# An attention-and-MLP kernel on one core: tail products take PSUM banks in the order of their release, and the list scheduler adds a constant to its assumed cost of every query/key eviction

## The chip, the cores and the metric

The kernel runs on one core of a Trainium2 chip. The metric is the device time of one execution in microseconds (us). A comparison is made in rounds in which both kernels run on the same chip. Each run is listed with the mean clock that the throttle granted to TensorE; 1.000 is full speed. A run over 1.5% above the fastest of its kernel is "slow"; a ratio compares fast runs alone, a median is over all runs. Engine names are those of the profile: PE is TensorE's matmul, PEld its weight load, ACT is ScalarE, DVE is VectorE. L1109 means line 1109 of the kernel.

## The reference, cut to what matters

```python
x: (1, 2048, 640), H = 32 heads of 20
xn  = layernorm(x)
q, k, v = split(xn @ wqkv)                       # 640 x 1920
p   = softmax(q @ k^T * 20**-0.5)                # 32 x 2048 x 2048 exponentials
s   = (p @ v) @ wo                               # 640 x 640
h   = layernorm(xn)
y   = gelu(h^T @ w1 + b1) @ w2 + b2              # mixes along the sequence, F = 1536
out = x + s * silu(y^T)
```

## The kernel before: the parts that the change and the argument touch

The kernel is not written in instruction order. A list scheduler, run when the kernel is built, deals all steps to the engines. It keeps a clock for each engine, reckoned with assumed costs. At each turn it asks every engine for candidates (priority, ready time, action), takes the engine whose next candidate is ready first, and emits that engine's candidate of lowest priority number. The compiled program is the resulting fixed list.

First, the costs decide which engine gets an eviction ("ev" step), and in which order everything after it is dealt:

```python
def dv(n, rate=1.04):  return 75.0 + n * rate          # believed DVE cost, ns
def ac(n):             return 90.0 + n * 0.833 + 60.0  # believed ACT cost, ns

def do_step(j, eng):
    s = j.steps[j.i]; j.i += 1
    if s[0] == "ev":
        n = s[8]; fn = ev_fn(s, eng)
        cost = ac(n) if eng == "act" else dv(n, 0.55 if s[7].startswith("xTe") else 1.04)
        getattr(pr, eng)(fn, reads=s[5], writes=s[6], name=s[7], cost=cost)
    # ... matmul steps and the rest
```

Second, PE's candidates. A score block (L1109: two 512-wide matmuls of 32 rows for one exponential, often with a third for a DVE chain) has priority 0. Filler work (value products L755, query/key chunks L722, MLP products L810, output products L879) has 30 and more. Attention-value products (L1224) have 8.

Third, the tail. The last two output blocks (`LBS`) are accumulated in PSUM banks named in advance, and each product waits for "its" bank to come free:

```python
BA, BB = (5, 7), (4, 0)          # bank of the 512-wide part, bank of the 128-wide part
for i, b in enumerate(LBS):
    add_job(f"tpa{i}", ... op_mms(b, ps(BA[i]), 0, 512, bank_slot[BA[i]], True, False) ..., rq + (f"bankoff{BA[i]}",), 60.0 + i)
    add_job(f"tpb{i}", ... op_mms(b, ps(BB[i], 128), 512, 128, ...) ..., rq + (f"bankoff{BB[i]}",), 60.0 + i)
...
if not bankq and 7 not in busybanks and 7 not in bank_off:
    bank_off.add(7); done.add("bankoff7")          # the same for the ACT and DVE banks
```

## Time and profile before

| what | before | how it is read |
|---|---|---|
| time, median of six runs | 867.07 us (866.84 to 868.54) | the runs taken beside the changed kernel |
| profiled span, clock | 865.0 us, 1.000 | page, list of cores |
| start of the 27th exponential | 46.19 us | timeline of ACT |
| **middle**: from there to the end of the last exponential | 809.2 us | 855.38 - 46.19 |
| **end**: from there to the end of the span | 9.6 us | 865.0 - 855.38 |

The three stretches add up to the span, so every difference between two kernels has one of three addresses. The words "start", "middle" and "end" are used in this sense throughout. The lines that carry these numbers stand in the prediction.

### The profile page before, as it was taken

How to read it: one execution, taken by the hardware profiler on the slowest of the kernel's cores; microseconds unless marked ns; L12 is line 12 of the kernel's file. 1: busy time of each engine (PE TensorE's matmuls, PEld its weight loads, DVE VectorE, ACT ScalarE, POOL GpSimd, SP SyncE). 2: the span in 40 equal slices, each digit the busy share in tenths (PEclk: the TensorE clock that was granted, in tenths of full speed). 3: DMA queues.
4: the chain of work that ended last, by engine and by line, in shares of the span. 5: the costliest groups of instructions: out<-in, count | busy, mean ns of one | idle time of the engine just before them, and what ended most of it. 6: DMA issues, size and time to landing. Idle time of an engine off the chain costs nothing.

```text
span 865.0 us, 16498 instructions
## 1 busy us (share of the span) xinstructions
PE 797.6 (92%) x5828; PEld 256.1 (30%) x5918; DVE 823.6 (95%) x2047; ACT 845.4 (98%) x925; POOL 14.0 (2%) x23
## 2 busy tenths in 40 slices
PE   8899999999999999999999999999899998998997
PEld 5422222222222223222322222222222222232233
DVE  8989999999999999999999999999999999999996
ACT  7899999999999999999999999999999999999996
POOL 3200000000000000000000000000000000000000
PEclk9999999999999999999999999999999999999999
DMA  8141010011010323010013022123312201042111
GB/s 236 48 113 30 9 35 10 16 36 31 11 55 14 77 36 88 11 55 10 16 25 78 23 51 52 25 52 71 67 30 46 47 11 11 3 102 69 41 39 41
DMA packets 123350, 39.32 MB, mean 45 GB/s; under 512 B 84312, under 2 KB 122152, under 8 KB 123272
## 3 DMA queue, kind: packets, MB, share of 16 engines
q1 hardware_dynamic: 123272, 38.27, 19.4%
q8 instruction: 50, 0.82, 0.4%
q14 instruction: 28, 0.23, 0.1%
HBM read 25.88 MB, written 9.83 MB: 41 GB/s over the span
## 4 chain that ended last, share of the span: by engine, by line
ACT 87%; PE 9%; DVE 2%; POOL 1%; issue 1%; ACTq 0%; POOLq 0%
ACT pt_sb L1137 85%; PE ps_all L1109 3%; PE ps_all L1224 1%; ACT zt_sb L843 1%; PE ps_all L755 1%; PE ps_all L879 1%; ACT zt_sb L838 1%; PE ps_all L1704 1%; DVE ew_sb L1177 0%; PE ps_all L683 0%; PE ps_all L722 0%; POOL v_sb L1298 0%; PE ps_all L703 0%; DVE dpt_sb L1183 0%; PE ps_all L658 0%
## 5 line engine op out<-in xcount | busy, mean ns | idle before, releaser
L1137 ACT ACTIVATE pt_sb<-ps_all 128x1024 bf16<-128x1024 f32 x888 | 819.9, 1147 | 3.6 <-PE ps_all L1109 3.0
L1109 PE MATMUL ps_all<-qk_sb 32*128 32x512 bf16 (+1 forms) x2112 | 367.8, 377 | 48.3 <-ACT pt_sb L1137 36.7
L1177 DVE TENSOR_SCALAR ew_sb<-ps_all 128x512 uint16<-128x512 uint16 x272 | 184.2, 684 | 20.7 <-PE ps_all L1109 19.6
L1109 PEld LDWEIGHTS ps_all<-qk_sb 32*128 32x128 bf16 x2112 | 97.1, 91 | 347.0 <-ACT pt_sb L1137 299.9
L1183 DVE SCALAR_TENSOR_TENSOR dpt_sb<-ps_all,el_sb 128x512 uint16<-128x512 f32 x272 | 182.0, 684 | 1.8
L1224 PE MATMUL ps_all<-pt_sb,v_sb 128*32 128x512 bf16 (+1 forms) x1833 | 162.6, 378 | 0.3 <-issue 0.3
L1181 DVE TENSOR_TENSOR el_sb<-ev_sb,el_sb 128x512 bf16<-128x512 bf16 x272 | 111.0, 417 | 1.1
L1182 DVE TENSOR_TENSOR el_sb<-el_sb,ew_sb 128x512 bf16<-128x512 bf16 x272 | 110.2, 417 | 0.9
L1224 PE MATMUL ps_all<-dpt_sb,v_sb 128*32 128x512 bf16 (+1 forms) x279 | 83.7, 379 | 0.0
L810 PE MATMUL ps_all<-regB,regA 128*128 128x128 bf16 (+1 forms) x371 | 75.6, 300 | 2.9 <-issue 1.1
L1178 DVE TENSOR_SCALAR ev_sb<-ew_sb 128x512 bf16<-128x512 uint16 x272 | 75.3, 285 | 2.3
L810 PE MATMUL ps_all<-regC,regA 128*128 128x128 bf16 (+1 forms) x370 | 74.2, 300 | 1.8 <-issue 1.0
L1179 DVE TENSOR_SCALAR el_sb<-ew_sb 128x512 bf16<-128x512 uint16 x272 | 75.1, 284 | 0.0
L722 PE MATMUL ps_all<-xnT_sb,wqk_sb 128*112 128x512 bf16 x200 | 68.2, 405 | 0.4 <-DVE zt_sb L816 0.4
L1224 PEld LDWEIGHTS ps_all<-pt_sb,v_sb 128*32 128x32 bf16 x1833 | 35.4, 94 | 55.6 <-issue 50.2
L1696 PE MATMUL ps_all<-wrm_sb 128*128 128x512 bf16 (+1 forms) x117 | 34.0, 376 | 3.9 <-DVE ps_all L513 2.2
L810 PEld LDWEIGHTS ps_all<-regB,regA 128*128 128x128 bf16 x384 | 25.8, 97 | 39.1 <-issue 24.0
L810 PEld LDWEIGHTS ps_all<-regC,regA 128*128 128x128 bf16 x384 | 25.0, 97 | 39.8 <-issue 28.1
L1704 PE MATMUL ps_all<-wrm_sb,v_sb 128*128 128x512 bf16 x97 | 34.0, 385 | 1.3 <-issue 0.7
L755 PE MATMUL ps_all<-wv_sb,xnT_sb 128*128 128x160 bf16 (+1 forms) x160 | 33.7, 303 | 0.4 <-DVE pk_sb L1030 0.3
L879 PE MATMUL ps_all<-wo_sb,xnT_sb 128*128 128x128 bf16 (+3 forms) x151 | 30.2, 298 | 1.1 <-issue 0.5
L722 PEld LDWEIGHTS ps_all<-xnT_sb,wqk_sb 128*112 128x112 bf16 x200 | 20.7, 127 | 30.5 <-issue 13.4
(89 smaller groups left out, 354.4 us busy)
## 6 DMA issues: line engine op xcount, KB each, us to landing
regA<-in_B_w_dram SPq DMA_DIRECT2D x6, 1024.0 KB
regA<-in_B_w_dram SPq DMA_DIRECT2D x8, 768.0 KB
qkT_scratch_dram<-pk_sb SPq DMA_DIRECT2D x40, 112.0 KB
qk_sb<-qkT_scratch_dram SPq DMA_DIRECT2D x56, 80.0 KB
regA<-in_A_x_dram SPq DMA_DIRECT2D x6, 640.0 KB
on_scratch_dram<-on_sb SPq DMA_DIRECT2D x124, 20.0 KB
out_dram<-regC SPq DMA_DIRECT2D x3, 640.0 KB
wqk_sb<-in_A_wqkv_dram SPq DMA_DIRECT2D x2, 680.0 KB
```

The lines of the kernel that those rows point to most:

```text
L722: steps.append(("pe", lambda e, dc=dc: e.matmul(ps_all[0:112, bk * 512:(bk + 1) * 512], wqk_sb[:, dc * 1280 + c0:dc * 1280 + c0 + 112], xn ...
L810: steps.append(("pe", lambda e, k=k: e.matmul(ps(bk, n), wap[:, k, col0:col0 + 128], rows[:, k, c0:c0 + n], start=(k == 0), stop=(k == nk ...
L1109: pr.pe(lambda e, outp=outp, lhsT=lhsT, rhs=rhs, g=g: e.matmul(outp, lhsT, rhs, start=True, stop=True, tile_position=(32 * g, 0)), reads=q ...
L1137: tk = pr.act(lambda e: e.activation(outp, inp, AF.Exp, bias=-self.OFFS * math.log(2.0) / 128.0, scale=math.log(2.0) / 128.0), reads=[bank ...
L1177: (lambda e: e.tensor_scalar(w3, lo, 0x7FFF, None, ALU.bitwise_and), bs, [sw], dv(N)),
L1178: (lambda e: e.tensor_scalar(v_, w_, 1.0 / 256.0, -128.0, ALU.mult, ALU.add), [sw], [sv], dv(N, .26)),
L1179: (lambda e: e.tensor_scalar(l_, w_, a3 / 65536.0, (b3 - 64.0 * a3) / 256.0, ALU.mult, ALU.add), [sw], [sl_], dv(N, .26)),
L1181: (lambda e: e.tensor_tensor(l_, v_, l_, ALU.mult), [sv, sl_], [sl_], dv(N, .52)),
L1182: (lambda e: e.tensor_tensor(l_, l_, w_, ALU.mult), [sl_, sw], [sl_], dv(N, .52)),
L1183: (lambda e: e.scalar_tensor_tensor(o_, zr, -(self.OFFS - 16256.0), l_, ALU.add, ALU.add), bs + [sl_], [S_(f"dpt{s0 + i}") for i in range( ...
L1224: pr.pe(lambda e, outp=outp, lhsT=lhsT, rhs=rhs, k=k, g=g: e.matmul(outp, lhsT, rhs, start=(k == 0), stop=(k == NB - 1), tile_position=(0, ...
L1704: pe_full(lambda e: e.matmul(ps(AB), zero, wrm_sb[:, P:P + 512], start=new, stop=new), [S_("warm"), S_("v_ones")], [sl_acc], "warmz", 512)
```

## The change

It has two parts. **Tail banks**: the tail products no longer wait for named banks; each takes the next bank that comes free. **Cost**: a query/key eviction is reckoned 130 ns dearer, on either engine. For 512 columns that makes 707 ns on ACT, where the trace of before has a record of 784 (at 30.00 us, with the next operation queued behind it, that one starts 661 ns later), and 737 on DVE, where it has 810. The intent is a shorter tail and a start in which evictions go to the engine that is really free.

```diff
-        BA, BB = (5, 7), (4, 0)
+        tbank = []
 ...
-            add_job(f"tpa{i}", (... op_mms(b, ps(BA[i]), ...)), rq + (f"bankoff{BA[i]}",), 60.0 + i)
+            add_job(f"tpa{i}", (... op_mms(b, ps(tbank[2 * i]), ...)), rq + (f"tbank{2 * i}",), 60.0 + i)
 ...
+        def bank_out(b):
+            bank_off.add(b)
+            tbank.append(b)
+            done.add(f"tbank{len(tbank) - 1}")
 ...
                 cost = ac(n) if eng == "act" else dv(n, 0.55 if s[7].startswith("xTe") else 1.04)
+                if s[3] in ("q", "k"):
+                    cost += 130.0
 ...
-                    bank_off.add(7)
-                    done.add("bankoff7")
+                    bank_out(7)
```

(Cut: the same replacement of `BA`, `BB` by `tbank` in the last steps of each block, and of `bank_off.add` by `bank_out` for the other banks.)

More of the change, by code (lines that the diff above doesn't have):

```diff
@@ L1456, in schedule @@
             add_job(f"stl{b0}", storel_steps(b0, nb), tuple(f"res{b}" for b in range(b0, b0 + nb)), 30.0)
-        BA, BB = (5, 7), (4, 0)
+        tbank = []
         def tail_fin(i):
             b = LBS[i]
-            steps = op_mms(b, ps(BA[i]), 0, 512, bank_slot[BA[i]], False, True)
-            steps += op_mms(b, ps(BB[i], 128), 512, 128, bank_slot[BB[i]], False, True)
+            steps = op_mms(b, ps(tbank[2 * i]), 0, 512, bank_slot[tbank[2 * i]], False, True)
+            steps += op_mms(b, ps(tbank[2 * i + 1], 128), 512, 128, bank_slot[tbank[2 * i + 1]], False, True)
             z = ztmp(i)
             g = regC[:, b, :]
-            steps.append(("act", lambda e: e.activation(z[:, 512:640], ps(BB[i], 128), AF.Copy), [bank_slot[BB[i]]],
+            steps.append(("act", lambda e: e.activation(z[:, 512:640], ps(tbank[2 * i + 1], 128), AF.Copy), [bank_slot[tbank[2 * i + 1]]],
                           [S_(f"z{i}_1")], f"tz{b}b", ac(128)))
             if i == 0:
-                steps.append(("dve", lambda e: e.tensor_tensor(g[:, 0:512], ps(BA[i]), g[:, 0:512], ALU.mult),
-                              [bank_slot[BA[i]], S_(f"g{b}")], [S_(f"r{b}_0")], f"tp{b}a", dv(512)))
+                steps.append(("dve", lambda e: e.tensor_tensor(g[:, 0:512], ps(tbank[2 * i]), g[:, 0:512], ALU.mult),
+                              [bank_slot[tbank[2 * i]], S_(f"g{b}")], [S_(f"r{b}_0")], f"tp{b}a", dv(512)))
                 steps.append(("dve", lambda e: e.tensor_tensor(g[:, 512:640], z[:, 512:640], g[:, 512:640], ALU.mult),
@@ L1473, in tail_fin @@
             else:
-                steps.append(("act", lambda e: e.activation(z[:, 0:512], ps(BA[i]), AF.Copy), [bank_slot[BA[i]]],
+                steps.append(("act", lambda e: e.activation(z[:, 0:512], ps(tbank[2 * i]), AF.Copy), [bank_slot[tbank[2 * i]]],
                               [S_(f"z{i}_0")], f"tz{b}a", ac(512)))
@@ L1485, in schedule @@
             rq = oTall[NTB - 1] + ("wo", f"a2_{b}")
-            add_job(f"tpa{i}", (lambda bk, i=i, b=b: op_mms(b, ps(BA[i]), 0, 512, bank_slot[BA[i]], True, False) + [
-                ("tag", f"tpa{i}")]), rq + (f"bankoff{BA[i]}",), 60.0 + i)
-            add_job(f"tpb{i}", (lambda bk, i=i, b=b: op_mms(b, ps(BB[i], 128), 512, 128, bank_slot[BB[i]], True, False) + [
-                ("tag", f"tpb{i}")]), rq + (f"bankoff{BB[i]}",), 60.0 + i)
+            add_job(f"tpa{i}", (lambda bk, i=i, b=b: op_mms(b, ps(tbank[2 * i]), 0, 512, bank_slot[tbank[2 * i]], True, False) + [
+                ("tag", f"tpa{i}")]), rq + (f"tbank{2 * i}",), 60.0 + i)
+            add_job(f"tpb{i}", (lambda bk, i=i, b=b: op_mms(b, ps(tbank[2 * i + 1], 128), 512, 128, bank_slot[tbank[2 * i + 1]], True, False) + [
+                ("tag", f"tpb{i}")]), rq + (f"tbank{2 * i + 1}",), 60.0 + i)
             add_job(f"tfin{i}", (lambda bk, i=i: tail_fin(i)),
                     (f"tpa{i}", f"tpb{i}", f"epL{len(self.QSPLIT) - 1}", f"x2_{NTB - 1}"), 10.0 + i)
+        def bank_out(b):
+            bank_off.add(b)
+            tbank.append(b)
+            done.add(f"tbank{len(tbank) - 1}")
         act_banks = [b for g in self.ACT_GROUPS for b in g]
@@ L1721, in schedule @@
                     if b not in bank_off and not any(b in x[1] for x in pexp):
-                        bank_off.add(b)
-                        done.add(f"bankoff{b}")
+                        bank_out(b)
                 if not bankq and 7 not in busybanks and 7 not in bank_off:
-                    bank_off.add(7)
-                    done.add("bankoff7")
+                    bank_out(7)
             for dg in self.DVE_GROUPS:
@@ L1731, in schedule @@
                         if b not in bank_off:
-                            bank_off.add(b)
-                            done.add(f"bankoff{b}")
+                            bank_out(b)
             activate()
```

## The prediction

(Cut, where marked: statements on the hardware that no trace of this case shows, and with them the conclusion that the added 130 ns are right for ACT, which rested on the author's estimate of 706 ns alone; the trace of before has 661 ns from start to start. No term of the forecast's sum is cut: it came to -2.5 + 0.5 - 0.9 = -2.9 us, or 864.0 us. The "about 0.30" of the 160-wide eviction is an estimate that agrees with the trace of before, where query/key evictions on ACT take 784 ns at 512 columns and 458 at 128, or 0.85 ns per column, and 572 - 320 x 0.85 is 300; in after it took 337.)

> **What bounds the kernel now.** I read the page first: the busy shares, then the chain of waits. The two lines of busy time and chain:
>
> ```profile
> PE 797.6 (92%) x5828; PEld 256.1 (30%) x5918; DVE 823.6 (95%) x2047; ACT 845.4 (98%) x925; POOL 14.0 (2%) x23
> ...
> ACT 87%; PE 9%; DVE 2%; POOL 1%; issue 1%; ACTq 0%; POOLq 0%
> ...
> L1137 ACT ACTIVATE pt_sb<-ps_all 128x1024 bf16<-128x1024 f32 x888 | 819.9, 1147 | 3.6 <-PE ps_all L1109 3.0
> ```
>
> ScalarE (ACT) is the bound: 845.4 of 865.0 us busy, 819.9 of them in 888 exponentials, and the chain is 87% ACT. A mean of 1147 ns counts overlap twice: in the undisturbed stretch from 159.94 to 241.74 us the chain has 89 of them in 81.80 us, so one costs **0.919 us**. So there are only 865.0 - 845.4 = **19.6 us** to win without removing ACT work. Where do they lie? The timeline of ACT alone gives it, first at the start:
>
> ```profile
> 25.08 1.93 ACT L1137 ACTIVATE pt_sb<-ps_all 128x1024 bf16<-128x1024 f32 x2
> 27.27 2.85 ACT L1137 ACTIVATE pt_sb<-ps_all 128x1024 bf16<-128x1024 f32 x3 [0.25 <-PE ps_all L1109]
> 30.00 0.79 ACT L1036 ACTIVATE qk_sb<-ps_all,cst_sb 128x512 bf16<-128x512 f32 x1
> 30.66 0.62 ACT L1029 ACTIVATE xnT_sb<-ps_all 128x512 bf16<-128x512 bf16 x1
> 32.62 0.78 ACT L1036 ACTIVATE qk_sb<-ps_all,cst_sb 128x512 bf16<-128x512 f32 x1 [1.35 <-PE ps_all L703]
> 33.88 5.71 ACT L1137 ACTIVATE pt_sb<-ps_all 128x1024 bf16<-128x1024 f32 x6 [0.48 <-PE ps_all L1109]
> ...
> 43.13 1.02 ACT L1137 ACTIVATE pt_sb<-ps_all 128x1024 bf16<-128x1024 f32 x1 [0.49 <-PE ps_all L1109]
> 44.05 0.57 ACT L1029 ACTIVATE v_sb<-ps_all 128x480 bf16<-128x480 f32 x1
> 44.51 1.03 ACT L1137 ACTIVATE pt_sb<-ps_all 128x1024 bf16<-128x1024 f32 x1
> ```
>
> (start, duration, engine, line, operation; in brackets the idle time before it and who ended it.) Between the 16th exponential (ends 30.12) and the 17th (starts 33.88) ACT does 3.76 us without one: it evicts a query block nobody waits for yet, then a transposed block of x, which TensorE (PE) needs for the next key block; PE computes that block while ACT idles 1.35 us; ACT evicts it. The 27th exponential starts at 46.19 after a further idle 0.65. From there to the last, at 855.38, ACT is practically gapless: 862 exponentials at 0.919 plus 14 tanh at 1.15 are 808.3 of 809.2 us. The other place is the end, in the chain of waits in order of time:
>
> ```profile
> 857.84 0.70 PE ps_all L879 x7
> 858.54 0.38 PE ps_all L884 x2
> 858.92 0.05 issue
> 858.97 1.13 PE ps_all L879 x4
> 860.10 0.39 PE ps_all L884 x2
> 860.49 0.02 issue
> 860.51 0.28 ACT zt_sb L1466
> ```
>
> (start, duration, engine, tile, line.) L884 is the last accumulation step of an output block, which needs the final attention result ("stage", written by VectorE, DVE, at 857.61 + 0.45 = 858.06). After the first such pair, PE still makes the five 512-wide L879 steps of the very last block, 1.13 us, although they don't depend on the stage: their bank, 7, comes free late. So 9.6 us pass from the last exponential to the end.
>
> [...]The query/key eviction has two pointers (scale and bias):[...] the trace has 784[...]; the scheduler reckons 90 + 427 + 60 = 577, with the change 707.[...] On DVE it reckons 607 and the trace has 810.[...] the L884 pair at 860.10 stands behind the 1.13 us of L879 that do not need the stage.[...] The trace shows that DVE's read of bank 7 (the 256-column L907) ends at 858.37, before the tail block in it begins at 858.97[...] The trace has 2.67 us from DVE's last instruction (862.33) to the end; the change leaves this.
>
> **The change, part by part.** No arithmetic is added or removed. The built program has the same 888 exponentials and the same 272 six-step DVE chains; only dummy warm-up matmuls go from 236 to 242 of 512 columns. The one engine assignment that moves is that of evictions in the start, because the list scheduler gives each step to whichever engine it believes is free first.
>
> *Start.* In the built order ACT loses two 480-wide value evictions (0.57 each), one x eviction (0.62) and one 512 query eviction (0.78), and gains one 256-wide query/key eviction (0.56) and one 160-wide value eviction (about 0.30: the 480-wide one less 320 columns). ACT busy: -2.54 + 0.86 = **-1.7 us**. DVE gets that work and is not the bound there: it waits several times before its first chain at 46.22.
> Step a, the gap before the 17th exponential: the query eviction and the x eviction are now on DVE, and 16 exponentials are followed by one key eviction alone. After the last score matmul PE does 4 transposes, 8 value products and a warm-up (0.17 + 0.6 + 0.25 = 1.0), then 5 key matmuls (1.1): 2.1 after that score block, which itself ends about 1.4 before exponential 16 does. So ACT waits 0.7, then eviction 0.75, then score and handover 0.5: 1.95 in place of 3.76, **-1.8**. Against it stand the two evictions that came earlier in the row less the one that left: 0.56 + 0.30 - 0.57 = +0.3. Net **-1.5**.
> Step b, exponentials 17 to 24: 8.0 us before for 7.4 of work; PE has much the same filling work: **0**. The wait at the next key block stays: **0**.
> Step c, exponentials 25 to 27: before, a value eviction (0.5 after overlap) and the wait of 0.65, since 8 value products stood ahead of the score; now the eviction is on DVE and the scores come before the products: **-1.0**, taking 0.15 for a new small wait.
> Sum of the start: **-2.5 us**.
>
> *Middle.* Same instructions, other order. It has under 1 us of slack now, so it can only lose: I allow **+0.5**.
>
> *Tail.* In the built order the products of both narrow final blocks and the first wide one no longer wait for banks 4/5/7/0 by name; after the last value products PE does 2 wide steps (0.45), 5 narrow (0.41), the 5 wide steps of the last block (1.13): 2.0 us, while DVE makes the stage (1.6). Then the first L884 pair, 5 narrow steps (0.41 by 8 in 0.66), the second pair. So between the pairs 0.41 stands instead of 1.13: -0.7. And ahead of the last value products PE has 10 narrow steps and one wide where it had 5 wide: about -0.2. Sum **-0.9 us**.
>
> Total -2.5 + 0.5 - 0.9 = **-2.9 us**, so 866.93 - 2.9 = **864.0 us**.
>
> **The rivals.** First, the middle gets worse: the change reshuffles thousands of lines of PE and DVE order, and a badly placed chain stalls ACT by a few tenths, several times. For it: DVE is 95% busy and PE 92%, so buffers are tight. Against: the waits of ACT on scores are 3.0 us in 7 places, nearly all in the start, so two banks in turn cover such shuffles. It would make 865 to 868. Second, the start gain is eaten: the wait for the transposed x block remains because DVE now does the query eviction (0.81) ahead of it. Then step a gives -0.7 in place of -1.5, and the total is about 865. Third, DVE becomes the bound at the start: its first chain comes later, and fewer exponentials are ready. Against: its count of chains is unchanged and PE's wait is on ACT (299.9 us of weight loads waited for it). Fourth, the tail is hidden anyway: if the stage comes later than PE is ready, the -0.7 shrinks to the difference of 2.0 and 1.6, a small loss of it. About 864.5.
>
> **Range and chances.** All rivals together move some 3 us each way. The floor of the span is near 845.4 - 1.7 of busy ACT, plus its idle times before the first exponential (0.72, 1.52, 1.14, 1.53, 0.41, 0.26, 0.27: 5.9) and in the tail (3.58 + 1.28 + 3.72 = 8.6, less 0.9): 857.3; and 2% is 17 us, which neither side can reach without the bound changing. I take 861.5 to 867.0 as the range; the same within 2% is all but sure.
>
> **What would show it.** In the new profile: 888 exponentials, ACT busy near 843.7; the 17th exponential near 32.3 us; the 27th near 43.7; the last ending near 853.4; 8.7 us from there to the end, with only narrow L879 steps between the two last pairs. Wrong if ACT's idle time between 50 and 850 us exceeds 2 us, if the 17th starts at 33 or later, or if the end still takes 9.5 us.

## More of the kernel before

**Dummy** matmuls (L1696 and L1704 in this kernel, L1704 and L1712 after the change; 512 columns, results thrown away) are there to hold the granted clock: 1.000 in the profiled run of this kernel. They get priority -1, ahead of the scores, when the scheduler's own reckoning of recent PE columns runs short. And when that reckoning says that the clock is already low (`warm` is false), filler jumps to -2.

```python
class _Gate:
    W = ...; TH = 2800.0
    def at(self, t):
        while t >= self.end:
            self.warm = self.acc >= self.TH        # columns streamed in the last window
            ...
WARM_FLOOR = 3600.0; PACE_FROM = 90.0; PACE_TO = 1825.0

# in pe_cands():
c.append((0.0, r, lambda grp=grp, us=us: do_st(grp, us)))                  # scores
rf = max(T, pr.gate.short_at(T, self.WARM_FLOOR, pr.gate.W - self.WARM_PRE))
if rf < r:
    c.append((-1.0, max(rf, ...), lambda wb=wb: warm_step(wb, 512)))       # forced dummy
for j in active:                                                           # filler
    c.append((j.prio if pr.gate.warm or not self.WARM else -2.0, ..., lambda j=j: do_step(j, "pe")))
release_paced(self.PACE_FROM, self.PACE_TO)   # spreads filler jobs over this range of score blocks
```

The window `W`, the threshold `TH` and the floor are the scheduler's own assumptions; no run here shows by what rule the chip grants the clock.

## The result, and the profile after

The changed kernel took **868.20 us** (median of six, 867.72 to 868.55) against 867.07 before. The ratio is 1.001, 95% interval 0.9997 to 1.0023. Here and below a ratio is the mean time of one kernel's fast runs over that of the other's fast runs of the same rounds, so it is not quite the ratio of the medians. The time lies outside the predicted range of 861.5 to 867.0. The profiled ones of both kernels had a clock of 1.000.

The profile page of the changed kernel (busy time and share, number of instructions; the chain; the group of the exponentials):

```profile
PE 796.8 (92%) x5835; PEld 258.2 (30%) x5924; DVE 825.5 (95%) x2049; ACT 845.9 (98%) x923; POOL 14.0 (2%) x23
...
ACT 71%; PE 17%; DVE 10%; issue 1%; POOL 1%; ACTq 0%; POOLq 0%; DVEq 0%
...
L1137 ACT ACTIVATE pt_sb<-ps_all 128x1024 bf16<-128x1024 f32 x888 | 821.4, 1123 | 5.5 <-PE ps_all L1109 4.5
```

The busy shares are those of before, to a tenth of a per cent for ACT. But ACT's share of the chain fell from 87% to 71%, the difference went to PE and DVE, and the mean record of an exponential fell from 1147 to 1123 ns. A *shorter* record is a bad sign here: it suggests that fewer exponentials were already queued behind the one before (one that starts after ACT idled has a record of 1.02 us, the median from the 27th on is 1.15 before). The start, from ACT's timeline of the changed kernel:

```profile
19.77 10.33 ACT L1137 ACTIVATE pt_sb<-ps_all 128x1024 bf16<-128x1024 f32 x11
31.27 0.78 ACT L1036 ACTIVATE qk_sb<-ps_all,cst_sb 128x512 bf16<-128x512 f32 x1 [1.17 <-PE ps_all L703]
32.53 2.96 ACT L1137 ACTIVATE pt_sb<-ps_all 128x1024 bf16<-128x1024 f32 x3 [0.48 <-PE ps_all L1109]
35.92 4.88 ACT L1137 ACTIVATE pt_sb<-ps_all 128x1024 bf16<-128x1024 f32 x5 [0.43 <-PE ps_all L1109]
40.72 0.78 ACT L1036 ACTIVATE qk_sb<-ps_all,cst_sb 128x512 bf16<-128x512 f32 x1
41.98 2.98 ACT L1137 ACTIVATE pt_sb<-ps_all 128x1024 bf16<-128x1024 f32 x3 [0.48 <-PE ps_all L1109]
45.41 6.60 ACT L1137 ACTIVATE pt_sb<-ps_all 128x1024 bf16<-128x1024 f32 x7 [0.45 <-PE ps_all L1109]
```

The query and the x eviction that stood ahead of the 17th exponential are gone from ACT; one key eviction is left there. The 17th starts at 32.53 (before: 33.88) and the 27th, the last of the row at 41.98, at 43.94 (before: 46.19). So far the change does what it was meant to do. But the 28th comes late (45.41, after ACT idled 0.45; before: 47.11), so that one exponential on, 1.70 us of the gain is left. By the border chosen above, this wait is counted in the middle.

In ACT's timeline from 60 us on, a row is broken where ACT idles for 0.15 us or more. Four of the broken places in the kernel after:

```profile
126.32 3.11 ACT L1137 ACTIVATE pt_sb<-ps_all 128x1024 bf16<-128x1024 f32 x3 [0.32 <-PE ps_all L1109]
129.89 104.79 ACT L1137 ACTIVATE pt_sb<-ps_all 128x1024 bf16<-128x1024 f32 x114 [0.46 <-PE ps_all L1109]
...
773.19 55.27 ACT L1137 ACTIVATE pt_sb<-ps_all 128x1024 bf16<-128x1024 f32 x60 [0.37 <-PE ps_all L1109]
828.83 28.92 ACT L1137 ACTIVATE pt_sb<-ps_all 128x1024 bf16<-128x1024 f32 x31 [0.38 <-PE ps_all L1109]
```

and the only one of that size after 60 us in the kernel before, with its last row:

```profile
482.02 14.77 ACT L1137 ACTIVATE pt_sb<-ps_all 128x1024 bf16<-128x1024 f32 x16 [0.48 <-PE ps_all L1109]
...
765.97 89.41 ACT L1137 ACTIVATE pt_sb<-ps_all 128x1024 bf16<-128x1024 f32 x97
```

The last 97 exponentials of before run in one row; after the change the same stretch is broken twice. The end, from the chain of waits after:

```profile
858.36 0.40 PE ps_all L1224 x7
858.76 2.42 PE ps_all L879 x12
861.18 0.38 PE ps_all L884 x2
861.55 0.38 PE ps_all L879 x5
861.94 0.39 PE ps_all L884 x2
```

Between the two L884 pairs, 0.38 stands where 1.13 stood. The account of the span:

| | before | after | difference | predicted |
|---|---|---|---|---|
| 27th exponential starts | 46.19 | 43.94 | -2.25 | -2.5 |
| middle | 809.2 | 813.8 | **+4.6** | **+0.5** |
| end | 9.6 | 8.7 | -0.9 | -0.9 |
| profiled span | 865.0 | 866.5 | +1.5 | -2.9 |

**Where in the middle.** I took the start time of every exponential from both traces. An exponential that finds its scores ready starts 0.904 us after the one before (the median; 0.903 before). I call an interval a *stall* if ACT idled over 0.02 us in it, and charge it what it has beyond 0.904. Before had **10 stalls, which cost 3.6 us; after has 23, which cost 8.4**. That is +4.8; all other intervals together are 0.2 us better. So the whole middle loss is 13 more stalls of 0.2 to 0.6 us each. The idle time itself grew only from 1.3 to 4.0 us, because a stall costs more than its idle time: the exponential before it has run to its end without the next one overlapping, and 1.02 us of record less 0.904 of spacing is another 0.12 us at the least. At 418.97 us ACT idles 0.07 us, which the timeline doesn't even break a row for, and the exponential is 0.39 us late.

In 12 of the 23 stalls (5.2 us) PE's order has dummies among the work between 2.0 and 0.35 us ahead of the late exponential; in 11 (3.3 us) only filler and value products. Before it was 8 (3.2 us) and 2 (0.4 us), so most of the stalls that came new have no dummy there. This is a count of what stood there, not yet a cause.

### The profile page after: what moved, and what is told of

It reads as the page before. It is cut to its first block, busy times and chain, and to the rows that moved or that the text cites. A ratio compares the mean times of both kernels' runs of the same rounds, so it can differ in the third digit from the quotient of the medians.

```text
span 866.5 us, 16539 instructions
## 1 busy us (share of the span) xinstructions
PE 796.8 (92%) x5835; PEld 258.2 (30%) x5924; DVE 825.5 (95%) x2049; ACT 845.9 (98%) x923; POOL 14.0 (2%) x23
## 4 chain that ended last, share of the span: by engine, by line
ACT 71%; PE 17%; DVE 10%; issue 1%; POOL 1%; ACTq 0%; POOLq 0%; DVEq 0%
ACT pt_sb L1137 69%; PE ps_all L1109 6%; PE ps_all L1224 3%; DVE ew_sb L1177 2%; PE ps_all L810 2%; DVE dpt_sb L1183 2%; DVE el_sb L1182 1%; DVE el_sb L1181 1%; PE ps_all L755 1%; PE ps_all L879 1%; PE ps_all L1704 1%; DVE ev_sb L1178 1%; PE ps_all L1712 1%; DVE el_sb L1179 1%; PE ps_all L722 1%
## 5 line engine op out<-in xcount | busy, mean ns | idle before, releaser
L1137 ACT ACTIVATE pt_sb<-ps_all 128x1024 bf16<-128x1024 f32 x888 | 821.4, 1123 | 5.5 <-PE ps_all L1109 4.5
L1109 PE MATMUL ps_all<-qk_sb 32*128 32x512 bf16 (+1 forms) x2112 | 364.0, 377 | 52.4 <-ACT pt_sb L1137 39.4
L1109 PEld LDWEIGHTS ps_all<-qk_sb 32*128 32x128 bf16 x2112 | 96.1, 91 | 342.0 <-ACT pt_sb L1137 292.6
L1224 PE MATMUL ps_all<-dpt_sb,v_sb 128*32 128x512 bf16 (+1 forms) x279 | 81.2, 379 | 0.0
L1704 PE MATMUL ps_all<-wrm_sb 128*128 128x512 bf16 (+1 forms) x142 | 43.1, 384 | 5.2 <-DVE ps_all L513 2.2
L879 PE MATMUL ps_all<-wo_sb,xnT_sb 128*128 128x512 bf16 (+2 forms) x152 | 29.5, 298 | 0.8 <-issue 0.3
L1712 PE MATMUL ps_all<-wrm_sb,v_sb 128*128 128x512 bf16 x77 | 27.9, 386 | 0.6 <-DVE tr_sb L1274 0.2
```

What stands on the lines that cost most here:

```text
L1109: pr.pe(lambda e, outp=outp, lhsT=lhsT, rhs=rhs, g=g: e.matmul(outp, lhsT, rhs, start=True, stop=True, tile_position=(32 * g, 0)), reads=q ...
L1137: tk = pr.act(lambda e: e.activation(outp, inp, AF.Exp, bias=-self.OFFS * math.log(2.0) / 128.0, scale=math.log(2.0) / 128.0), reads=[bank ...
L1224: pr.pe(lambda e, outp=outp, lhsT=lhsT, rhs=rhs, k=k, g=g: e.matmul(outp, lhsT, rhs, start=(k == 0), stop=(k == NB - 1), tile_position=(0, ...
L1704: pe_full(lambda e: e.matmul(ps(wb, n), wrm_sb[:, 0:P], wrm_sb[:, P:P + n], start=True, stop=True), [S_("warm"), S_("warm1")], [bank_slot[ ...
```

## The experiments

Theories at the outset. **Redealing**: the new cost is used only for query/key evictions, of which the last comes at about 92 us, but it alters the scheduler's clocks, and everything later is dealt in another order; that order stalls ACT more often. **Payback**: PE and DVE work skipped in the start must be done later, so the gain of the start is given back in any case. **Tail banks**: that part has its own effect in the last microseconds and maybe none elsewhere. Later the question became which property of the order makes the stalls. Sixteen kernels ran; all gave correct results. Where the clock of a profiled run dropped, the text says so, and only the part before the drop is compared: late scores at a lower clock say nothing about the order (at a clock of 0.50, narrow28_late starts 19 exponentials in 25 us where after starts 28).

### One part at a time: tail_only and cost_only

```diff
 tail_only (the changed kernel with)      cost_only (the kernel before with)
-                    cost += 130.0        +                if s[3] in ("q", "k"):
+                    cost += 0.0          +                    cost += 130.0
```

> The kernel before with the tail banks in order of release alone (the added cost is 0). Built order: identical to before up to the last microseconds. Both theories: 17th exponential at 33.9 us, 27th at 46.2, middle (27th exponential to the end of the last) 809.2 as before; from the end of the last exponential to the end of the span 8.7 in place of 9.6 if the tail term of the prediction is right, so about 866.1 us by the clock; unchanged, about 867.0, if the tail is hidden.

> The kernel before with the added 130 ns alone. Both theories: the start of the changed kernel (27th exponential at 43.9) and its long middle (about 813.9). If the tail banks matter, the end takes 9.6 us and the time is about 869; if the reordering alone gives the short tail, it is the changed kernel's 868.2.

tail_only: 866.90 us (866.57 to 867.22), ratio 0.9994 (0.9982 to 1.0007): **nothing**. 27th exponential at 46.26, middle 809.1, end 9.6, ten stalls costing 3.5 us. Its chain at the end:

```profile
857.85 1.18 PE ps_all L879 x6
859.03 0.27 PE ps_all L884 x2
859.31 0.81 PE ps_all L879 x6
860.11 0.39 PE ps_all L884 x2
```

Between the pairs 0.81 replaced 1.13, as bank order should do, but the first pair moved from 858.54 to 859.03, and PE is done at 860.50 as it was at 860.49. The end is bound by the sum of PE's remaining work; which of it stands between the pairs is of no account.

cost_only: 868.52 us (867.95 to 871.54), ratio 1.0018 (1.0000 to 1.0036): **the whole change**. 27th at 43.90, end 8.7 without any change of the banks. Its profiled execution (870.79, clock 0.995) had a dip of the clock between 675 and 700 us (0.86), so its middle of 816.1 isn't comparable. But between 120 and 600 us it has the same 14 stalls as the changed kernel, one by one, from 126.28 (for 126.32) to 541.77 (for 541.82), each within 0.1 us of the time and 0.03 us of the size. Two executions of one order stall in the same places: the stalls belong to the order, not to chance.

So the cost alone makes the start's gain and the middle's loss and comes with the shorter end, and the bank part is without effect.

### Another order with the same start: floor3500, gate2600, before_floor3300

Three kernels change a constant of the dummies: how many columns the scheduler wants in a window before it forces a dummy (floor), or from how many it believes the clock high (gate).

```diff
 floor3500 (after)             gate2600 (after)          before_floor3300 (before)
-    WARM_FLOOR = 3600.0      -    TH = 2800.0           -    WARM_FLOOR = 3600.0
+    WARM_FLOOR = 3500.0      +    TH = 2600.0           +    WARM_FLOOR = 3300.0
```

> The changed kernel with the scheduler's floor for forced dummy matmuls at 3500 columns in place of 3600: start unchanged, 24 fewer dummies of 512 columns, another order in the middle. Payback theory (the engines besides ACT are the true limit of the first 150 us, so what the start gains is lost again whatever the order): middle stays near 813.9, time near 868. Order theory (the middle's loss lies in the particular list that the scheduler fell into, above all in dummies ahead of scores): middle back to 809 or less, time 863 to 864, faster than both kernels.

> The changed kernel with the scheduler's threshold for believing the TensorE clock low at 2600 columns in place of 2800: the one interval in the middle (around 126 us) in which it believed so, and put value products ahead of the scores, goes away; start unchanged. Order theory: the 1.6 us lost between the 107th and the 147th exponential come back (0.3 lost there), middle near 812 or less, time 866 to 867. Payback theory: the loss appears elsewhere before the 150th exponential, time 868.

> The kernel before with the floor at 3300 (38 fewer dummies of 512 columns). Start as before (27th at 46.2). If the before kernel's middle was already as good as it gets, it stays at 809; if fewer dummies help whatever the start, 808 or less; tail about 9; time 864.5 to 866.5. If the floor's gain in the other run came by way of the changed start alone, 867.

| | 27th | middle | end | stalls: number, us | time, us | ratio (95%) |
|---|---|---|---|---|---|---|
| before | 46.19 | 809.2 | 9.6 | 10, 3.6 | 867.07 | |
| after | 43.94 | 813.8 | 8.7 | 23, 8.4 | 868.20 | 1.001 (0.9997 to 1.0023) |
| floor3500 | 43.52 | 810.6 | 8.8 | 9, 3.0 | **864.73** | **0.997 (0.9957 to 0.9983)** |
| gate2600 | 43.80 | 812.5 | 9.0 | 13, 4.2 | 867.07 | 1.0028 (0.9989 to 1.0066) |
| before_floor3300 | 46.18 | 808.5 | 9.2 | 6, 1.7 | 866.10 | 0.9978 (0.9965 to 0.9992) |

(Every profiled clock is 0.999 or 1.000. gate2600 had two runs at clocks of 0.982 and 0.992, 878.43 and 872.22, which widen its interval. The deal also moves one or two units between ACT and DVE: floor3500 and before_floor3300 have 889 exponentials, gate2600 890, so their middles hold 0.9 or 1.8 us more work; for equal work they would be 809.7, 807.6 and 810.7.)

**Payback falls as a general rule.** floor3500 keeps the whole gain of the start and of the end, its middle holds one more exponential, and it has 9 stalls instead of 23. It has 218 dummies of 512 columns where after has 242, so it alone can't tell another order from less work for PE. gate2600 can: with its 246 dummies it has 13 stalls, and pace_to1823 below has 14 with 249. That a part of the start's gain is paid back is not excluded: for equal work none of these deals with the new start has a middle as short as the 809.2 of before. floor3500 is the best kernel, at 864.73 us (864.59 to 865.02); its interval lies below 1 and below that of after. That this is close to the 864.0 predicted for the change is chance: it is another list. The same kind of edit gains a little on the kernel before too, 0.2%.

**gate2600 explains one piece.** PE of the kernel after, between 125 and 130 us:

```profile
125.17 0.78 PE L755 MATMUL ps_all<-wv_sb,xnT_sb 128*128 128x480 bf16 x3
125.89 0.64 PE L1109 MATMUL ps_all<-qk_sb 32*128 32x512 bf16 x4
...
128.93 0.59 PE L1712 MATMUL ps_all<-wrm_sb,v_sb 128*128 128x512 bf16 x2 [0.16 <-DVE dpt_sb L1183]
129.46 0.39 PE L1109 MATMUL ps_all<-qk_sb 32*128 32x512 bf16 x3
```

Three value products stand ahead of the scores, though filler has the higher number: in the built schedule this is a place where the reckoned columns of a window fell just under the threshold of 2800 (2720, in the window that ends at 122.9 us by the scheduler's own time; the kernel before has no such window after the first), so the scheduler believed the clock low and let filler pass. The granted clock there was 1.00 (125 to 150 us). Four stalls at 126.32, 128.40, 129.89 and 148.36 cost 1.6 us. With the threshold at 2600 the same stretch of ACT is one unbroken row (seen in the window from 120 to 132 us):

```profile
118.97 13.28 ACT L1137 ACTIVATE pt_sb<-ps_all 128x1024 bf16<-128x1024 f32 x14
```

All four stalls are gone, and up to the 347th exponential the loss against after is 1.6 us smaller: **1.6 of the 4.8 us** came from a false alarm of the scheduler's model. (What gate2600 gains after that is another deal.)

### Unrelated small changes: pace85, pace_to1823, floor3400_pace100, floor3450_to1815

If the order is what counts and before's was simply a good one, any small edit of the deal should move the middle by microseconds.

```diff
 pace85: PACE_FROM 90 -> 85          pace_to1823: PACE_TO 1825 -> 1823
 floor3400_pace100: WARM_FLOOR 3600 -> 3400, PACE_FROM 90 -> 100
 floor3450_to1815:  WARM_FLOOR 3600 -> 3450, PACE_TO 1825 -> 1815      (all in the kernel after)
```

> The changed kernel with the first paced job released at unit 85 in place of 90, a change that has nothing to do with query/key evictions or tail banks: start instruction for instruction the same, another order in the middle. Lottery theory (any small change of the scheduler's inputs deals a new middle): the middle moves by 1 us or more from 813.8, and I expect it worse, 815 to 818, since the scheduler believes in a low clock for one interval and lets fillers pass; time 869 to 872. Theory that the added cost is what harms the middle: middle within 0.5 of 813.8.

> The changed kernel with paced jobs released up to unit 1823 in place of 1825, nothing else: same instructions, same start, as many dummies within a few. Lottery theory: the middle moves by 1 us or more from 813.8; the scheduler's own reckoning has it 2.7 us shorter, so 810.5 to 812.5, time 866 to 867.5. Theory that the added cost harms the middle: within 0.5 of 813.8.

> The changed kernel with floor 3400 and the first paced job at unit 100: chosen as the best draw of a few dozen. Start as the changed kernel (27th exponential at 43.5 to 43.9), tail 8.7 to 8.9. Lottery and dummy theory: middle 808 to 810, time 862 to 864, faster than both kernels and no slower than the floor at 3500 (864.7). Payback theory: 867 to 868.

> The changed kernel with floor 3450 and paced jobs released up to unit 1815: the draw with the earliest end by the scheduler's own reckoning of some sixty, with more dummies than the one at floor 3400. Order theory: start 43.5 to 43.9, middle 809 to 811, tail 8.8 to 9.3, time 863.5 to 865.5, faster than both kernels; where the clock dips in some executions, 866 or more in those.

pace_to1823 moves the release of filler by two score blocks in 1,825. At a clock of 1.000 its middle is 812.2, with one exponential more, and 14 stalls (5.7 us) for after's 813.8 with 23. It keeps the four stalls of the false alarm; after the 347th exponential it has 6 (2.5 us) where after has 15 (5.3 us), with more dummies. Two of four runs took 867.25 and 867.53, a third 868.57, and one took 876.37 at a clock of 0.986. pace85 was worse: 870.89 us, ratio 1.0039 (1.0021 to 1.0057), middle 816.2, part of which is a stretch at clock 0.93 between 125 and 150 us: 4.6 us are lost there (107th to 147th exponential) for 1.7 in after, so it doesn't show a worse order. The two kernels chosen to do better than floor3500 missed. floor3400_pace100: 868.60 us, from 866.64 to 885.73, with clocks of 0.964 to 0.997. floor3450_to1815: 869.27 us, ratio 1.0021 (1.0009 to 1.0034), only one of five runs above a clock of 0.994 (866.91). In that one the order is nearly free of stalls, 2 that cost 0.8 us, but for the 3.0 us that it loses near 815 us, where the clock falls (0.93 from 800 to 825). The number of dummies doesn't tell: 218 of 512 columns kept the clock at 0.999 to 1.000 in six runs (floor3500), and 222 in another order had 0.992 to 0.998 in five (floor3450_to1815). So fewer dummies are a gain only while the clock holds, and which deals hold it I could not foretell.

### Are the dummies themselves the stall? narrow_dummies, narrow28_late, narrow28_other

In many stalls dummies stand ahead of the late scores. narrow_dummies makes every forced dummy 64 columns wide (112 of the 242). narrow28_late narrows only 28 that stand ahead of late exponentials; narrow28_other, the control, 28 neighbours that don't.

```diff
 narrow_dummies                                         narrow28_late / narrow28_other
-   lambda wb=wb: warm_step(wb, 512)                   +   NARROW = (33, 34, 52, 53, 54, 89, ...)  # / (35, 36, 50, ...)
+   lambda wb=wb: warm_step(wb, 512, 64)               +   m = 64 if ndum[0] - 1 in NARROW else n
```

(The 0.19 us per dummy in the next two texts is an estimate. The trace of after has 0.226 us from the start of a 512-wide dummy to that of a second right behind it; 448/512 of that is 0.198.)

> The changed kernel, every instruction in the same place with the same waits, but the 112 dummy matmuls that the scheduler forces ahead of other work are 64 columns wide in place of 512 (it still reckons them as 512). Dummy theory (half the middle's loss is dummies that stand in front of a score block): each saves 0.19 us of TensorE where a score waits behind it; middle 811 to 812.5 in place of 813.8, unless the granted clock falls below 0.99, which would show what they are for and lengthen all. Order theory without dummies (the loss is which scores stand behind which products): middle unchanged within 0.5.

> The changed kernel, every instruction in the same place with the same waits, but 28 dummy matmuls are 64 columns wide in place of 512: those that stand directly ahead of the score blocks whose exponential started 1.16 us or more after the one before. Dummy theory: those late starts lose about 0.19 us per narrowed dummy where the score truly waited; 12 such places with 2 or 3 dummies, so the middle falls from 813.8 by 2 to 4 us to 810 to 812 and the time to 864.5 to 866.5, if the clock stays at 0.998 or more. If those dummies only fill time in which the score could not have run anyway, the middle stays at 813.8. If the clock falls, the affected stretch shows it.

> The control: 28 other dummies, neighbours of those in the list, with no late exponential next to them, made 64 wide in the changed kernel. Dummy theory: nothing to win there; middle 813.3 to 814, time 868 (more where the clock falls). If narrowing 28 dummies anywhere gives the same gain as the other run, it is not the place ahead of the late scores that counts.

narrow_dummies: **904.27 us**, ratio 1.043, at a clock of 0.928. The clock row of its page, in 40 slices of the span (9 is full):

```profile
PEclk9999999999999999999958998999997655699999
```

With 112 dummies narrowed the clock fell in all four runs (0.917 to 0.931), and the question couldn't be asked in this way. With 28 the clock holds until about 400 us in the profiled executions of both kernels (that of narrow28_late is slow, for what comes later), so the part before can be compared: reckoned from the 27th exponential on, the 347th is late against 0.915 us per exponential and 1.14 per tanh by 3.48 us in after, **2.73** in narrow28_late, 3.45 in the control. (cost_only, the same order in another execution, has 3.47, so these numbers repeat to some hundredths.) Five narrowed dummies lie in this part; narrowing them is worth 0.75 us, and the control's 0.03. The clearest case is the three dummies ahead of the stall at 129.89 (the profile of after shows two; the third record is missing). ACT of narrow28_late there (window from 118 to 136 us):

```profile
125.97 10.50 ACT L1137 ACTIVATE pt_sb<-ps_all 128x1024 bf16<-128x1024 f32 x11 [0.32 <-PE ps_all L1109]
```

The break before (0.32) remains, as it comes from the value products. The one of 0.46 has gone.

Beyond 400 us the clock falls in the profiled executions of both, and the mean clock is under 0.995 in 9 of the 12 runs: 873.07 us (866.87 to 884.42) and 877.41 us (868.16 to 885.84), medians; the ratios of the fast ones are 1.0035 and 1.0088. The best ones, at clocks of 0.998 and 1.000, are 866.87 and 868.16. A stretch of 25 us, narrow28_late first, then after (window; its length; busy us and instructions of PE, PEld, DVE, ACT, POOL; clock; DMA share; GB/s):

```profile
425.00:450.00 25.00, 25.00 (x124) 5.73 (x122) 17.52 (x44) 18.73 (x19) 0.00 (x0) 0.50 0.06 18
```

```profile
425.00:450.00 25.00, 23.50 (x177) 7.36 (x177) 24.20 (x60) 24.80 (x28) 0.00 (x0) 1.00 0.11 22
```

At half clock PE is the bound: busy for the whole 25.00 us, it does 124 matmuls for 177, and ACT 19 exponentials for 28. And though it is busy without a gap, its clock stays at half through the window.

### Is it where they stand? behind28, behind28_other, behind_all, floor3500_behind_all

What was still open: whether it is the dummy's *time* or its *place* ahead of the scores. A pass over the finished PE list moves dummies behind the score block that follows them; all else stays.

```diff
+    def scores_first(self):
+        out, hold, ndum = [], [], -1
+        for t in self.prog.tasks["pe"]:
+            if t.name in ("warm", "warmz"):
+                ndum += 1
+                if ndum in self.BEHIND:            # behind_all: every dummy
+                    hold.append(t)
+                    continue
+            if not t.name.startswith("st"):        # not a score matmul
+                out += hold
+                hold = []
+            out.append(t)
+        ...
```

(The 0.27 us there: in after two dummies ahead of a score take 0.54 us of PE, from 433.10 to 433.64.)

> The changed kernel; after the list is made, the 28 full-width dummies that stand directly ahead of the score blocks of late exponentials are moved directly behind those blocks. Nothing else moves, all waits and widths are kept. Dummy theory: a dummy takes about 0.27 us of the queue ahead of the score, so the 12 places with 1 to 4 dummies give back most of their lateness: middle from 813.8 to 810.5 to 812, time 865 to 866.5, at a clock of 0.999 or 1.0. If the rest of the loss is not of the dummies: middle 813 to 814, time 868.

> The control: 28 other dummies, where no exponential near them was late, moved behind the score blocks that follow them. Dummy theory: the exponentials there did not wait, so middle 813.3 to 814.2 and time 868. If it gains as much as the other run, the place does not matter.

> The changed kernel with every dummy that stands directly ahead of a score block moved behind it (153 places). Dummy theory: at least the gain of the 28, with some given back where the dummy filled time in which the score could not run: middle 810 to 812.5, time 865 to 867.

> The kernel with the floor at 3500 (864.73 us, middle 810.6), with the same move. If dummies ahead of scores are what is left of its middle loss: middle 809 to 810, time 863.5 to 864.5; if the late starts left there are of products, 864.7 within 0.4.

behind28 (the same 28 dummies): 874.85 us, ratio 1.0095. In its profiled execution the clock holds until 375 us (0.86 from there to 400), and the 347th exponential is 3.75 us late, against 3.48 in after and 2.73 with the same dummies narrowed. **Moving them gains nothing.** The stall at 129.89 only comes one exponential later, with the same size (0.47; the three dummies take 0.75 us of PE there, 129.72 to 130.47; window from 60 to 160 us):

```profile
126.74 4.02 ACT L1160 ACTIVATE pt_sb<-ps_all 128x1024 bf16<-128x1024 f32 x4 [0.32 <-PE ps_all L1132]
131.24 29.58 ACT L1160 ACTIVATE pt_sb<-ps_all 128x1024 bf16<-128x1024 f32 x32 [0.47 <-PE ps_all L1132]
```

(L1160 and L1132 are L1137 and L1109 of the kernel after, moved by the inserted lines.) So the theory of the place fell. Where PE has no time to spare, as in this stretch, it is the dummy's PE time that is paid, before this block of scores or before the next. behind28_other took 869.20 us (868.85 to 875.09); its profiled execution has a stretch at clock 0.93 from 125 to 150 us and can't serve as a control for the stalls, so this test has none. behind_all: 924.90 us, and floor3500_behind_all 922.04 us, ratios 1.066 and 1.062, at clocks of 0.942 and 0.945: with all dummies moved, the clock falls in many places (behind_all has 14 stretches of 25 us below 1.00, the lowest 0.71, from 750 to 775) although their number and width are unchanged.

## Why the prediction was wrong, point by point

**The bound.** Right: ACT is busy 845.9 of 866.5 us, and PE and DVE did not take its place over the span. Its sign "ACT busy near 843.7" did not come, though: the start has 1.5 us less, nearly the 1.7 reckoned, but the middle 1.9 more with the same 888 exponentials and 14 tanh. Lateness without idle time counts as busy.

**Start, -2.5.** Right in mechanism and nearly in size: -2.25. Step a was sized -1.5 and measured -1.35 (17th at 32.53 for 33.88), by two errors that partly cancel: the gap from the end of the 16th shrank by 1.33 instead of 1.8, as ACT waited 1.17 for the key block and not 0.7, and the +0.3 ahead of it did not come (-0.02); step b 0 and +0.18 (17th to 24th: 7.26 for 7.08); step c -1.0 and -1.08 (24th to 27th: 4.15 for 5.23). The "new small wait" of 0.15 came as 0.45, one exponential later, and so is in the middle's sum.

**Middle, +0.5: the step that failed.** "Same instructions, other order. It has under 1 us of slack now, so it can only lose: I allow +0.5." It measured **+4.6**. The direction was right, and the first rival, "a badly placed chain stalls ACT by a few tenths, several times", describes what happened, and its own "865 to 868" came within 0.2 us of the 868.2, while the range that was given stopped at 867.0; the size of this term alone carries the miss, 4.1 of the 4.4 us by which the span was off. Two readings led there. First, the sum "862 exponentials at 0.919" took as the cost of an exponential a mean from a stretch that itself contains late ones (7 of the 88 intervals have over 0.95 us, none with idle over 0.02); the free spacing is 0.904, so before was not gapless but had ten stalls worth 3.6 us. Second, "the waits of ACT on scores are 3.0 us in 7 places, nearly all in the start" was taken as proof that two banks in turn cover a reshuffle. It showed only that *this* order was a good one. The waits in the new order, 4.5 us in 14 places, are again an understatement of the stalls. The allowance should have been several microseconds wide: at full clock, the deals tried here have between 6 and 23 stalls, 1.7 to 8.4 us.

Of the +4.8 us of stalls, 1.6 are shown to come from the scheduler's false belief in a low clock at 126 to 149 us (gate2600), of which about 0.5 is the time of three dummies within that stretch (narrow28_late); narrowing two more is worth some 0.2. By stretches the loss against before is 0.4 us up to the 107th exponential (where the 28th alone, late in every kernel with the new start, cost 0.57), 1.5 from there to the 147th, none to the 347th, and 2.7 after it. This last part is **not settled** stall by stall. It depends on the order, since cost_only repeats its stalls up to 600 us and pace_to1823, with the same stalls before it and more dummies, doesn't have it. Dummies stand ahead of a little over half of what the stalls there cost more than before, but every kernel that narrowed or moved the later ones lost its clock in its profiled run (means of 0.928 to 0.991).

**Tail, -0.9.** The size came out, but by other terms. "So between the pairs 0.41 stands instead of 1.13: -0.7" was attributed to the bank order; 0.38 does stand there, but tail_only shows that such a change is worth nothing, for what leaves the gap goes ahead of the first pair. From the end of the last exponential PE needs 4.57 us instead of 5.10, **-0.53**, and cost_only has the same 4.57: in the redealt list more of the last steps are done ahead of the last value products (4.00 us pass on PE behind them in before, 3.56 in after). That is the term which the prediction had as "about -0.2"; its own figures, 10 narrow steps (0.82) and one wide (0.23) for five wide (1.13), give -0.1. The -0.9 came out by luck. The other -0.36 is in the last transfer, which the prediction had as unchanged at 2.67 us: from DVE's last instruction to the end it takes 2.66 in before and 2.29 in after. before_floor3300, with the old banks and costs, has 2.29 too, so it doesn't need the change; its cause stays open.

**The other rivals.** The start's gain was not eaten, DVE did not become the bound of the start, and the tail was not hidden by the stage (in after, DVE ends it at 860.35, and PE is busy until the first pair at 861.18). **The wrong-if list** did its work: ACT's idle time between 50 and 850 us was to stay below 2 us, and is 3.35 (800 less 796.65 of busy time; before 1.29).

## What to carry to other kernels

Where a greedy scheduler deals a whole program, a corrected cost in its first tenth is a new draw for all the rest: the draw itself must be put in the range, from a few neighbouring builds, before a small local gain is credited. The scheduler itself can be asked: the recorded kernels, built again, give its own end of the program as 858.8 us for before, 861.4 for after, 856.5 for floor3500, 859.7 for gate2600 and 856.8 for before_floor3300, against profiled spans of 865.0, 866.5, 862.9, 865.3 and 863.9. It had the loss as +2.6, with the right sign, before any run; the prediction did not use it. It says nothing of the clock: for floor3400_pace100 it has 856.0, measured 866.9 at a clock of 0.994. Count late starts against the free spacing of the bounding engine rather than its idle time; here idle showed 2.7 us of a 4.8 us loss. And before moving work out of a gap on an engine, ask whether the sum of its remaining work bounds the end, in which case the order within it is worth nothing.
